# Moving the conversion of a weight chunk behind the next step's row turn after a small slot

## The chip, the core and the metric

The kernel runs on one core of a Trainium2 chip. The metric is the device time of one execution in microseconds (us). The engines work side by side, each through its own queue in order: TensorE (PE in the rows; PEld is its weight loading), VectorE (DVE), ScalarE (ACT), GpSimd (POOL) and SyncE (SP, which only issues DMA transfers here). "DVEq" and the like name an engine's sequencer: branches and semaphore events, not work.

## The reference, cut to what matters

Three stages follow each other: windowed attention, a top-1 mixture of experts (MoE) whose expert is sometimes held from one token to the next, and a gated feed-forward layer with a convolution. The change lies in the MoE stage and touches the weights of the third.

```python
# MoE: d_model 512, 8 experts, d_ff 1024, 4 x 544 tokens
e = fresh_e if s == 0 or local_gate[b, s] < 0.5 else prev_e
h = np.maximum(x[b, s] @ w1[e], 0.0)
out[b, s] = p[e] * (h @ w2[e])
# third stage
h = np.maximum(x @ w_in, 0.0)
gate = 1.0 / (1.0 + np.exp(-conv(h, conv_w)))
return h * gate @ w_out
```

The weights w_in and w_out (and conv_w) arrive with 8 bytes per number; the kernel brings them to 4-byte floats itself, with integer operations.

## The kernel before, in words

The MoE stage sorts the tokens by expert into **slots** of 128 rows; a slot holds one expert only. `Moe.run` (L1186) runs slots 2 to 20 by `step(s)` (L1406), one step per slot, and slot 21 by `last`. Every matmul is done in three products of high and low parts: a float tile is split into a high part (by ScalarE, a cast) and a low part (by VectorE, a subtraction). So a step on TensorE is: layer 1 of slot s, the row turn of slot s+1 (`turn_x`: four transposes; ScalarE writes xh, VectorE xl), layer 2 of slot s-1, the turn of the hidden rows of slot s (`turn_h`; ScalarE writes gh, VectorE gl).

Where the expert changes from slot s to s+1, its weights, loaded by SyncE into ws (`fetch`, L1280), are split: W1 by `resplit(s + 1, 1)` in step s (four pieces), W2 by `resplit(s + 1, 2)` at the end of step s+1 (eight pieces, W2 of slot s by `resplit(s, 2)` in step s). Both lie in a conditional block on `chg` of the slot (L1295), which every engine passes, taken or not; the registers come from the routing table `esi`, row 1. A slot with at most 32 rows is **small** (row 5 of `esi`): its two layers are computed straight from the unsplit weights and take TensorE about 2 us each in place of 5.6.

Beside this, sixteen **chunks** of the third stage's weights are converted, one a step. `raw_load` (L1442) brings chunk s-2 into one of two buffers in step s. Chunk c = s-3 is converted in step s by `conv64` (L1007): six operations on VectorE (L1011 to L1016), one addition on GpSimd (L1017), and a last operation on VectorE, here called the **tail** (L1018), which is returned as a function and run a step later, in the `while self.conv` loop right behind the row turn. Where the expert stays from s to s+1, the six operations stand early in the step (block of L1424, ahead of layer 2, the hidden turn and the W2 split); where it changes, at the step's end (block of L1436). The engines' queues follow the order in which the code is written; nothing reorders them.

In this data the slots with a changed expert are 4, 7, 9, 13, 16, 18 and 21; small slots that `step` runs are 2, 9, 13 and 16. After 9, 13 and 16 the next slot keeps the expert.

Of the kernel before, what the change touches and what calls it, by code (L numbers as in the profile page):

```python
# [13 lines left out]
ALU = mybir.AluOpType  # L14
# [545 lines left out]
NA = 2  # L560
NB = NSLOT - NA
# [94 lines left out]
class Routing:  # L656
# [15 lines left out]
    def tl(self, shape, name, dt=F32, tag=None):  # L672
        return self.rp.tile(shape, dt, name=name, tag=tag or name)
# [170 lines left out]
    def phase_b(self, rp, pst):  # L844
        nc, c, tl = self.nc, self.c, self.tl
        v = nc.vector
        self.rp = rp
        yield from self.front(1, pst)
        n = NT
# [40 lines left out]
        sc = tl([1, NB], "r_sc")  # L890
# [24 lines left out]
        esi = self.esi  # L915
        ch = tl([1, NB], "r_ch")
# [8 lines left out]
        va = tl([1, NB], "r_va")  # L925
# [4 lines left out]
        v.tensor_tensor(esi[:, 3, NA + 1:], va[:, 1:], ch[:, 1:], ALU.mult)  # L930
        v.tensor_scalar(esi[:, 2, NA:], ni, 7, None, ALU.bitwise_and)
        v.tensor_copy(esi[:, 4, 0:1], inc[0:1, 7:8])
        yield

    def few(self, b0, first):
# [71 lines left out]
def conv64(nc, raw, out):  # L1007
    hi, lo = raw[:, :, 1], raw[:, :, 0]
    v = nc.vector
    a = out.bitcast(I32)  # L1010
    v.tensor_scalar(a, hi, 3, 0x7FFFFFFF, ALU.logical_shift_left, ALU.bitwise_and)  # L1011
    v.scalar_tensor_tensor(a, hi, -2 ** 31, a, ALU.bitwise_and, ALU.bitwise_or)
    v.tensor_scalar(hi, hi, 1, 21, ALU.logical_shift_left, ALU.logical_shift_right)
    v.tensor_scalar(hi, hi, 897.0, -1.0, ALU.is_ge, ALU.mult)
    v.scalar_tensor_tensor(a, lo, 29, a, ALU.logical_shift_right, ALU.bitwise_or)
    v.tensor_scalar(lo, lo, 28, 1, ALU.logical_shift_right, ALU.bitwise_and)  # L1016
    nc.gpsimd.tensor_tensor(a, a, lo, ALU.add)  # L1017
    return lambda: v.scalar_tensor_tensor(a, a, 0x40000000, hi, ALU.bitwise_xor, ALU.bitwise_and)  # L1018
# [33 lines left out]
class Moe:  # L1052
    def __init__(self, sig, tc, W, ident, x_dram, y_dram, rt, w1, w2, wi, wo):
        self.nc, self.tc = tc.nc, tc
        self.W, self.ident, self.x_dram, self.y_dram = W, ident, x_dram, y_dram
        self.rt, self.w1, self.w2, self.wi, self.wo = rt, w1, w2, wi, wo
        self.sig = sig
        self.xs, self.xt, self.ht, self.hs, self.next, self.chg, self.sm = {}, {}, {}, {}, {}, {}, {}
        self.conv, self.raw = [], {}

    def open(self, ctx):
        self.ctx = ctx
# [146 lines left out]
    def last(self, s, cwr, cw):  # L1209
        nc, W, f2 = self.nc, self.W, self.f2  # L1210
        hp, hs = self.h_tile(), self.tp.tile([P, FF], F32, tag="hs", name="hs")
        xt, ht = self.xt.pop(s), {}
        w, y = W.t[1], {}
        ht = tuple(self.tp.tile([P, NFC, P], F32R, tag="g" + x, name="g" + x) for x in "hl")

        def split(a, b):
            for k in range(a, b):
                W.split_k(1, W.f, k, nc.gpsimd if k in POOL_K[1] else nc.vector)

        def resplit(a, b):  # L1220
            with self.tc.If(self.chg[s] != 0):
                for k in range(a, b):
                    W.split_k(2, W.s, k, nc.gpsimd if k in POOL_L else nc.vector)

        for k in range(K_LAST):
            self.l1_mm(xt, w, hp, k, range(2))
        split(0, K_LAST)
        nc.scalar.activation(self.sig, self.sig, AF.Sigmoid)
        self.layer2(s - 1)
        self.fetch(s - 1, 2)  # L1230
        f2.load0()
        resplit(0, 4)
        for k in range(K_LAST, NKC - 1):
            self.l1_mm(xt, w, hp, k, range(2))
        self.conv_w(cwr, cw)
        self.rt.late_flag(s + 1, self.ps.tile([P, 4, P], F32, tag="tr", name="lf")[0:1, 0, 0:1])
        t = []
        for c in range(2):
            self.l1_mm(xt, w, hp, NKC - 1, (c,))
            self.relu_c(hp, hs, c)  # L1240
        for a in (0, 4):
            t.append(self.hi_t(hs, ht, a, self.ps))
        for a in (0, 4):
            self.lo_t(ht, a, t[a // 4])
        resplit(4, NFC)
        yp = self.y_tile()
        for k in range(NFC):
            self.l2_mm(ht, W.t[2], yp, k)
            for f in PREP0.get(k, ()):
                if f < 10:  # L1250
                    (f2.scale0 if f < 5 else f2.xt0)(f % 5, self.ps)
                else:
                    split(f - 10, f - 9)
        self.out(s, yp)
# [30 lines left out]
        self.W.load(n, (self.w1, self.w2)[n - 1][bass.ds(e, 1)], **({"cond": c} if (s, n) != (0, 1) else {}))  # L1285

    def changed(self, s, pool=False):
        return self.nc.values_load(self.rt.esi[0:1, 1, s:s + 1], min_val=0, max_val=1,
                                   engines=[mybir.EngineType.Activation, mybir.EngineType.Pool]
                                   + ([] if pool else [mybir.EngineType.DVE]))  # L1290

    def resplit(self, s, n, eng=None):
        if n == 1 or s < NA:
            self.chg[s] = self.changed(s, eng is not None)
        with self.tc.If(self.chg[s] != 0):  # L1295
            self.W.split(n, self.W.s, eng)

    def small(self, s):
# [107 lines left out]
    def step(self, s):  # L1406
        W, hi = self.W, NSLOT - 3
        if s + 1 < hi - 1:
            self.small(s + 1)
        self.layer1(s)  # L1410
        self.fetch(s, 1)
        if s + 3 < hi:
            self.xs[s + 3] = self.gather(s + 3)
        if s + 1 < hi - 1:
            self.turn_x(s + 1)
        else:
            self.xt[s + 1] = self.hi_lo_t(self.xs.pop(s + 1), NKC, "x")
        while self.conv:
            self.conv.pop()()
        if s < NA + 16:  # L1420
            self.raw_load(s - NA)
        self.resplit(s + 1, 1)
        if NA < s <= NA + 16:
            with self.tc.If(self.chg[s + 1] == 0):  # L1424
                self.convert(s - NA - 1)
        if s == NA:
            for _ in self.rest:
                pass
        else:
            self.layer2(s - 1)  # L1430
            self.fetch(s - 1, 2)
        self.turn_h(s)
        self.resplit(s, 2)
        if NA < s <= NA + 16:
            self.conv.pop()
            with self.tc.If(self.chg[s + 1] != 0):  # L1436
                self.convert(s - NA - 1)

    def chunk(self, s):
        return (1, s // 2, 512 * (s % 2)) if s < 8 else (2, s - 8, 0)  # L1440
# [6 lines left out]

    def convert(self, s):
        n, k, o = self.chunk(s)
        self.conv.append(conv64(self.nc, self.raw[s], self.W.f[n][:, k, o:o + 512]))  # L1450


class Ffn2:
# [411 lines left out]
```

## Time and profile before

| | us |
|---|---|
| time, median of three runs | 630.27 (627.69 to 630.58) |
| profiled execution | 626.94 |
| its span | 624.9 |
| TensorE busy in the span | 579.3 (93%) |
| VectorE busy | 416.5 (67%) |
| ScalarE busy | 318.2 (51%) |
| GpSimd busy | 176.5 (28%) |

The steps of the MoE stage run from about 180 to 394 us of the span, `last` to about 416, and the third stage from about 421 on. Busy shares are means over stages with different limits: within a step it counts which engine another one waits for. A timeline row gives start, duration, engine, line, operation, output and inputs, and in brackets the idle time ahead of it and what ended it.

### The profile page before, as it was taken

To read this page: it belongs to the slowest core of one execution; us is meant where nothing else is said; L and a number is where in the kernel's file an instruction comes from. 1 tells how busy PE (TensorE), PEld (TensorE's weight loads), DVE (VectorE), ACT (ScalarE), POOL (GpSimd) and SP (SyncE) were. 2 spreads that over 40 slices of the span, in tenths; PEclk is the share of its full clock that TensorE was granted. 3 is DMA by queue.
4 is the path that set the end of the run, shared out by engine and by line. 5 is a ranking of instruction groups with operands and counts; after the bars stand their busy time and mean duration, and the time that the engine had idled before them with its cause. 6 is when DMAs were issued, how large, how long until landed. Compare 5 with 4: busy or idle time off the path is not lost. (4 is left out here: it accounts for less than half of the span.)

```text
span 624.9 us, 16315 instructions
## 1 busy us (share of the span) xinstructions
PE 579.3 (93%) x6066; PEld 484.7 (78%) x6066; DVE 416.5 (67%) x868; ACT 318.2 (51%) x634; POOL 176.5 (28%) x226
## 2 busy tenths in 40 slices
PE   8779898889989999989989899969999999999997
PEld 7567676666758888768767688749998998998986
DVE  7868577866965878784878884578984384383330
ACT  5755545574225455443545654656864463463341
POOL 7665820042031423333243330100132243300100
PEclk9999989999899999989999899998999999999999
DMA  9989968558049575774558474123101201000001
GB/s 232 208 172 263 258 127 196 201 178 287 20 128 335 206 242 205 250 255 162 216 172 289 158 254 153 38 75 85 50 15 37 85 2 50 35 2 35 34 35 51
DMA packets 60643, 90.56 MB, mean 145 GB/s; under 512 B 25726, under 2 KB 34198, under 8 KB 60504
## 3 DMA queue, kind: packets, MB, share of 16 engines
q1 hardware_dynamic: 57016, 78.93, 41.7%
q0 software_dynamic: 3520, 10.23, 4.8%
q8 instruction: 64, 1.05, 0.7%
q14 instruction: 43, 0.35, 0.2%
HBM read 125.87 MB, written 15.79 MB: 227 GB/s over the span
## 5 line engine op out<-in xcount | busy, mean ns | idle before, releaser
L1569 DVE SCALAR_TENSOR_TENSOR fc<-f_hp,cw,fc 128x544 f32<-128x544 f32 (+2 forms) x66 | 51.1, 775 | 70.7 <-ACT fc L1567 69.3
L1045 DVE TENSOR_TENSOR wl<-ws,wh 128x512 fp32r<-128x512 f32 (+1 forms) x92 | 74.3, 868 | 12.5 <-ACT wh L1044 11.8
L1044 ACT CAST wh<-ws 128x512 fp32r<-128x512 f32 (+1 forms) x96 | 66.3, 772 | 2.0 <-DMA ws<-in_moe_w_dram 0.9
L1125 PE MATMUL yp<-wh,gh 128*128 128x512 f32 x144 | 58.9, 409 | 1.1 <-ACTq L1295 0.9
L1125 PE MATMUL yp<-wl,gh 128*128 128x512 f32 x144 | 57.0, 396 | 0.7 <-DVEq L1295 0.7
L1125 PE MATMUL yp<-wh,gl 128*128 128x512 f32 x144 | 57.0, 396 | 0.0
L1109 PE MATMUL hp<-wl,xh 128*128 128x512 f32 x144 | 47.5, 402 | 8.6 <-DVEq L1295 5.4
L1627 PE MATMUL f<-wh,fh 128*128 128x512 f32 (+1 forms) x144 | 54.8, 380 | 0.0
L1627 PE MATMUL f<-wh,fl 128*128 128x512 f32 (+1 forms) x144 | 54.4, 378 | 0.0
L1627 PE MATMUL f<-wl,fh 128*128 128x512 f32 (+1 forms) x144 | 54.4, 378 | 0.0
L1082 POOL DMA_INDIRECT y_dram<-ys,sidx x22 | 25.4, 1156 | 95.8 <-ACT ys L1401 46.7
L1273 ACT ACTIVATE hs<-hp 128x512 f32<-128x512 f32 x36 | 19.9, 595 | 61.1 <-PE hp L1109 61.1
L278 ACT ACTIVATE pr<-sp,nm 128x128 f32<-128x128 f32 x128 | 36.6, 375 | 26.4 <-DVE nm L275 26.4
L1109 PE MATMUL hp<-wh,xh 128*128 128x512 f32 x144 | 49.2, 413 | 0.1
L1109 PE MATMUL hp<-wh,xl 128*128 128x512 f32 x144 | 47.8, 404 | 0.0
L1070 POOL DMA_INDIRECT xs<-x_dram,gidx x22 | 26.9, 1225 | 64.6 <-ACT pr L278 34.1
L1017 POOL TENSOR_TENSOR wf<-wf,fx 128x512 int32<-128x512 int32 x16 | 20.9, 1304 | 74.4 <-DVE fx L1016 66.0
L1109 PEld LDWEIGHTS hp<-wl,xh 128*128 128x128 f32 x144 | 27.2, 192 | 16.3 <-DVEq L1295 6.7
L1574 ACT ACTIVATE f_hp<-f 128x544 f32<-128x544 f32 x31 | 19.4, 626 | 36.8 <-PE f L1550 36.7
L1636 ACT COPY fy<-f 128x512 f32<-128x512 f32 (+1 forms) x18 | 10.1, 564 | 47.1 <-PE f L1627 47.1
L1401 ACT COPY ys<-yp 128x512 f32<-128x512 f32 x15 | 8.9, 592 | 48.7 <-PE yp L1125 42.4
L1109 PEld LDWEIGHTS hp<-wh,xl 128*128 128x128 f32 x144 | 27.7, 193 | 6.4 <-DVE xl L1102 0.3
(380 smaller groups left out, 1525.6 us busy)
## 6 DMA issues: line engine op xcount, KB each, us to landing
ws<-in_moe_w_dram SPq DMA_DIRECT2D x42, 2048.0 KB
fx<-y_dram SPq DMA_DIRECT2D x17, 256.0 KB
raw<-in_k_l_dram SPq DMA_DIRECT2D x16, 256.0 KB
x_dram<-x SPq DMA_DIRECT2D x16, 256.0 KB
fx<-in_moe_w_in_dram SPq DMA_DIRECT2D x8, 512.0 KB
fx<-in_moe_w_out_dram SPq DMA_DIRECT2D x8, 512.0 KB
out_dram<-fy SPq DMA_DIRECT2D x16, 256.0 KB
VA<-in_v_l_dram SPq DMA_DIRECT2D x20, 192.0 KB
```

The source lines that it names most:

```text
L278: nc.scalar.activation(pr[:, hp, :], sp[:, hp, :], AF.Exp, bias=nm[:, hp:hp + 1], scale=-1.0)
L1017: nc.gpsimd.tensor_tensor(a, a, lo, ALU.add)
L1044: (cp.tensor_copy if cp else self.nc.scalar.copy)(h, src[n][:, k, :])
L1045: eng.tensor_tensor(l, src[n][:, k, :], h.bitcast(F32), ALU.subtract)
L1070: self.nc.gpsimd.indirect_dma_start(out=xs, out_offset=None, in_=self.x_dram[0:n, :], in_offset=bass.IndirectOffsetOnAxis(ap=self.rt.gidx[ ...
L1082: self.nc.gpsimd.indirect_dma_start(out=self.y_dram[:, :], out_offset=bass.IndirectOffsetOnAxis(ap=self.rt.sidx[:, s:s + 1], axis=0), in_= ...
L1109: self.nc.tensor.matmul(hp[c], a[:, k, :], b[:, 512 * c:512 * c + 512], start=k == 0 and m == 0, stop=k == NKC - 1 and m == 2)
L1125: self.nc.tensor.matmul(yp, a[:, k, :], b, start=k == 0 and m == 0, stop=k == NFC - 1 and m == 2)
L1273: self.nc.scalar.activation(hs[:, 512 * c:512 * c + 512], hp[c], AF.Relu)
L1569: nc.vector.scalar_tensor_tensor(c[:, a:b], hp[:, a + t:b + t], self.cw[:, t, f:f + 1], c[:, a:b], ALU.mult, ALU.add)
L1574: self.nc.scalar.activation(hp[:, 1:S + 1].rearrange("p (a c) -> p a c", a=2), p[:, :, 0:272], AF.Relu)
L1627: self.nc.tensor.matmul(yp[:, cs], x[:, c], w[:, cs], start=f == 0 and n == 0, stop=f == NFC - 1 and n == 2)
```

## The change

The routing table's row 1 gets a third value: a slot that keeps its expert after a small slot that changed it has 2 (four operations on one partition at the end of `phase_b`). The blocks that split weights now ask for `== 1` in place of `!= 0`, so 2 counts as unchanged there.

The tail of a chunk moves from the loop behind the row turn into a new `convert_early`, behind `resplit(s + 1, 1)`. There, a step whose own value is 2 runs the whole conversion of the chunk before (six operations, addition, tail); any other runs the tail of the chunk before and then, as before, the six operations of its own chunk if `chg` of the next slot is 0. `convert_end` at the step's end runs the own chunk if `chg` of the next slot is 1 or the own value is 2. A small slot's step whose next slot has value 2 thus converts nothing. `raw_load` moves behind `convert_early`.

```diff
@@ phase_b
+        sc = tl([1, NB], "r_sc")
+        v.tensor_tensor(sc, ch, esi[:, 5, NA:], ALU.mult)
+        v.tensor_scalar(va, ch, -2.0, 2.0, ALU.mult, ALU.add)
+        v.tensor_tensor(sc[:, 0:NB - 1], sc[:, 0:NB - 1], va[:, 1:], ALU.mult)
+        v.tensor_tensor(esi[:, 1, NA + 1:], sc[:, 0:NB - 1], ch[:, 1:], ALU.add)
@@ resplit (and the same in last)
-        with self.tc.If(self.chg[s] != 0):
+        with self.tc.If(self.chg[s] == 1):
             self.W.split(n, self.W.s, eng)
@@ step
-        while self.conv:
+        while s > NA + 17 and self.conv:
             self.conv.pop()()
+        self.resplit(s + 1, 1)
+        self.convert_early(s)
         if s < NA + 16:
             self.raw_load(s - NA)
-        self.resplit(s + 1, 1)
-        if NA < s <= NA + 16:
-            with self.tc.If(self.chg[s + 1] == 0):
-                self.convert(s - NA - 1)
...
         self.turn_h(s)
         self.resplit(s, 2)
-        if NA < s <= NA + 16:
-            self.conv.pop()
-            with self.tc.If(self.chg[s + 1] != 0):
-                self.convert(s - NA - 1)
+        self.convert_end(s)
+
+    def convert_early(self, s):
+        c = s - NA - 1
+
+        def own():
+            if 0 <= c < 16:
+                with self.tc.If(self.chg[s + 1] == 0):
+                    self.convert(c)
+
+        if 0 < c <= 16:
+            with self.tc.If(self.chg[s] == 2) as i:
+                self.convert(c - 1)
+                self.tails[c - 1]()
+            with i.Else():
+                self.tails[c - 1]()
+                own()
+        else:
+            own()
+
+    def convert_end(self, s):
+        c = s - NA - 1
+
+        def own():
+            with self.tc.If(self.chg[s + 1] == 1):
+                self.convert(c)
+
+        if 0 < c < 16:
+            with self.tc.If(self.chg[s] == 2) as i:
+                self.convert(c)
+            with i.Else():
+                own()
+        elif c == 0:
+            own()
@@ convert
-        self.conv.append(conv64(self.nc, self.raw[s], self.W.f[n][:, k, o:o + 512]))
+        self.tails[s] = conv64(self.nc, self.raw[s], self.W.f[n][:, k, o:o + 512])
```

VectorE in a step before, behind the row turn (xl): wf is the converted chunk, fx its raw buffer, wl and ws the low part and the unsplit W1.

```order
L1102 TENSOR_TENSOR xl<-xlp,xh 128x512
L1304 UNCONDITIONAL_BRANCH
L1018 SCALAR_TENSOR_TENSOR wf_3965<-wf_3965,fx 128x512
L1288 TENSOR_LOAD esi
L1295 COMPARE_AND_BRANCH
L1045 TENSOR_TENSOR wl_0_2726<-ws_3447,wh_0_2725 128x1024
...
L1295 UNCONDITIONAL_BRANCH x2
L1424 COMPARE_AND_BRANCH
L1011 TENSOR_SCALAR wf_3965<-fx 128x512
```

The same place of the changed kernel, where lines stand five lower in the file:

```order
L1107 TENSOR_TENSOR xl<-xlp,xh 128x512
L1309 UNCONDITIONAL_BRANCH
L1293 TENSOR_LOAD esi
L1300 COMPARE_AND_BRANCH
L1050 TENSOR_TENSOR wl_0_2726<-ws_3447,wh_0_2725 128x1024
...
L1300 UNCONDITIONAL_BRANCH x2
L1448 COMPARE_AND_BRANCH
L1016 TENSOR_SCALAR wf_3970<-fx 128x512
...
L1021 TENSOR_SCALAR fx<-fx 128x512
L1023 SCALAR_TENSOR_TENSOR wf_3970<-wf_3970,fx 128x512
L1448 UNCONDITIONAL_BRANCH
L1023 SCALAR_TENSOR_TENSOR wf_3970<-wf_3970,fx 128x512
L1444 COMPARE_AND_BRANCH
```

The tail (L1018, now L1023) stands behind the block of the W1 split and twice: at the end of the put-off conversion (the block of L1448) and, in the other branch, alone ahead of the own conversion (L1444).

SyncE in a step before: the raw load (fx) ahead of the blocks, the W2 load (ws) behind them.

```order
L1446 DMA fx<-in_moe_w_in_dram 128x1024 [waits DMAHW7_49,DVE_49]
L1295 UNCONDITIONAL_BRANCH
L1424 UNCONDITIONAL_BRANCH
L1304 UNCONDITIONAL_BRANCH x2
L1037 ISA
L1037 DMA ws_2724<-in_moe_w_dram 128x8x512 [waits DMAHW3_49,PE_49,Activation_49]
```

And changed:

```order
L1300 UNCONDITIONAL_BRANCH
L1448 UNCONDITIONAL_BRANCH
L1309 UNCONDITIONAL_BRANCH x2
L1479 DMA fx<-in_moe_w_in_dram 128x1024 [waits DMAHW7_49,DVE_49,Pool_49]
L1042 ISA
L1042 DMA ws_2724<-in_moe_w_dram 128x8x512 [waits DMAHW3_49,PE_49,Activation_49]
```

The raw load now comes behind the conversion's block and waits for GpSimd too; the W2 load still follows it in the queue.

## Rows read from the trace of the kernel before

**Rows 1.** Timeline of TensorE: second matmul of layer 1, slots 11, 15, 18.

```profile
275.94 0.72 PE L1109 MATMUL hp<-wl,xh 128*128 128x512 f32 x2 [2.21 <-DVEq L1295]
...
321.69 0.73 PE L1109 MATMUL hp<-wl,xh 128*128 128x512 f32 x2 [2.09 <-DVEq L1295]
...
354.60 0.79 PE L1109 MATMUL hp<-wl,xh 128*128 128x512 f32 x2 [3.11 <-DVE wl L1045]
```

**Rows 2.** Table by stage: us, busy of each engine, then PEclk, DMA share, GB/s.

```profile
243.34:248.92 5.58, 5.58 (x27) 4.54 (x26) 5.01 (x9) 5.18 (x11) 1.98 (x2) 1.00 0.59 227
273.03:282.67 9.64, 7.43 (x25) 5.58 (x26) 6.14 (x11) 1.13 (x3) 2.32 (x2) 0.82 0.67 211
318.89:326.81 7.92, 5.83 (x25) 4.46 (x25) 6.03 (x11) 1.23 (x3) 1.61 (x2) 1.00 0.54 170
350.78:361.31 10.53, 7.42 (x25) 5.59 (x26) 8.60 (x11) 3.97 (x8) 1.41 (x1) 0.84 0.69 221
420.00:427.00 7.00, 6.13 (x28) 6.16 (x28) 5.50 (x10) 2.50 (x5) 0.28 (x6) 0.51 0.56 133
```

**Rows 3.** Timeline of VectorE, from step 9 into step 10.

```profile
264.28 0.43 DVE L1011 TENSOR_SCALAR wf<-fx 128x512 int32<-128x512 int32 x1 [0.41 <-DVEq L1295]
...
267.00 0.43 DVE L1016 TENSOR_SCALAR fx<-fx 128x512 int32<-128x512 int32 x1
267.99 5.59 DVE L1045 TENSOR_TENSOR wl<-ws,wh 128x512 fp32r<-128x512 f32 x8 [0.57 <-PE hp L1109]
274.54 0.69 DVE L1102 TENSOR_TENSOR xl<-xlp,xh 128x512 fp32r<-128x512 f32 x1 [0.95 <-ACTq L1295]
275.14 0.68 DVE L1018 SCALAR_TENSOR_TENSOR wf<-wf,fx 128x512 int32<-128x512 int32 x1
```

**Rows 4.** Timeline of GpSimd: the addition of the conversion in step 9.

```profile
267.51 1.30 POOL L1017 TENSOR_TENSOR wf<-wf,fx 128x512 int32<-128x512 int32 x1 [2.68 <-DVEq L1304]
```

**Rows 5.** Who waited for whom, TensorE, 165 to 425 us: total, times, longest.

```profile
PE yp L1125 <- DVEq L1295: 0.7, 1, 0.7
```

**Rows 6.** Timeline of TensorE: second matmul of layer 2, slots 10, 12, 15, 17.

```profile
283.34 0.40 PE L1125 MATMUL yp<-wl,gh 128*128 128x512 f32 x1
...
304.44 0.39 PE L1125 MATMUL yp<-wl,gh 128*128 128x512 f32 x1
...
336.30 0.39 PE L1125 MATMUL yp<-wl,gh 128*128 128x512 f32 x1
...
361.98 0.40 PE L1125 MATMUL yp<-wl,gh 128*128 128x512 f32 x1
```

**Rows 7.** Timeline of ScalarE: casts of W2 in step 9, of W1 in step 17.

```profile
265.57 4.27 ACT L1044 CAST wh<-ws 128x512 fp32r<-128x512 f32 x8 [0.73 <-DMA ws<-in_moe_w_dram]
...
348.74 3.90 ACT L1044 CAST wh<-ws 128x1024 fp32r<-128x1024 f32 x4
```

**Rows 8.** Timeline of SyncE: raw load and W2 load of step 8.

```profile
251.95 0.34 SPq L1446 DMA_DIRECT2D fx<-in_moe_w_in_dram  x1
255.14 3.21 SPq L1037 DMA_DIRECT2D ws<-in_moe_w_dram  x2
```

**Rows 9.** Timeline of VectorE: tail in step 8, gl in 12, W1 split in 17.

```profile
251.23 0.69 DVE L1018 SCALAR_TENSOR_TENSOR wf<-wf,fx 128x512 int32<-128x512 int32 x1 [1.22 <-DVEq L1304]
...
302.78 1.29 DVE L1102 TENSOR_TENSOR gl<-hlp,gh 128x512 fp32r<-128x512 f32 x2 [0.53 <-ACTq L1295]
...
353.32 4.62 DVE L1045 TENSOR_TENSOR wl<-ws,wh 128x1024 fp32r<-128x1024 f32 x4
```

**Rows 10.** Timeline of VectorE, steps 14 and 15: xl, tail, gl of slot 15.

```profile
320.29 0.69 DVE L1102 TENSOR_TENSOR xl<-xlp,xh 128x512 fp32r<-128x512 f32 x1 [0.95 <-ACTq L1295]
...
328.40 0.69 DVE L1018 SCALAR_TENSOR_TENSOR wf<-wf,fx 128x512 int32<-128x512 int32 x1 [1.91 <-POOLq L1424]
...
334.77 1.29 DVE L1102 TENSOR_TENSOR gl<-hlp,gh 128x512 fp32r<-128x512 f32 x2 [0.53 <-ACTq L1295]
```

**Rows 11.** Timeline of VectorE: xl of slot 2, behind the routing.

```profile
179.88 0.69 DVE L1102 TENSOR_TENSOR xl<-xlp,xh 128x512 fp32r<-128x512 f32 x1 [1.58 <-ACT xh L1327]
```

More of the change, by code (lines that the diff above doesn't have):

```diff
@@ L1058, in __init__ @@
         self.xs, self.xt, self.ht, self.hs, self.next, self.chg, self.sm = {}, {}, {}, {}, {}, {}, {}
-        self.conv, self.raw = [], {}
+        self.conv, self.raw, self.tails = [], {}, {}
     def open(self, ctx):
@@ L1287, in changed @@
     def changed(self, s, pool=False):
-        return self.nc.values_load(self.rt.esi[0:1, 1, s:s + 1], min_val=0, max_val=1,
+        return self.nc.values_load(self.rt.esi[0:1, 1, s:s + 1], min_val=0, max_val=2,
                                    engines=[mybir.EngineType.Activation, mybir.EngineType.Pool]
@@ L1294, in resplit @@
             self.chg[s] = self.changed(s, eng is not None)
-        with self.tc.If(self.chg[s] != 0):
+        with self.tc.If(self.chg[s] == 1):
             self.W.split(n, self.W.s, eng)
```

## Prediction

> **What bounds the kernel now.** The waits of TensorE in the expert stretch (165 to 425 us) were read first. The long ones all stand in front of the second matmul of a layer 1, the one that reads the low part of W1: 2.21 us at 275.94, 2.09 at 321.69 and 3.11 at 354.60 [rows 1]. These are layer 1 of slots 11, 15 and 18. Slots 9, 13 and 16 ran small: each of the three comes two steps after a small slot. That matmul may go only when VectorE has passed the row turn of its slot (xl) and the W1 split's block, taken or not.
>
> A table by stage then gives the price [rows 2]. An undisturbed layer 1 with its first turn takes 5.58 us; the three take 9.64, 7.92 and 10.53. The excess is 4.06 + 2.34 + 4.95 = 11.35 us, of which 7.41 is waiting. Most of the rest is clock: the first and third stretch were granted 0.82 and 0.84, so (1 - 0.82) x 9.64 = 1.74 and (1 - 0.84) x 10.53 = 1.68 us went to the lower level; the second ran at 1.00.
>
> What ends last is on VectorE. In step 9 [rows 3] it converts chunk 6 (six operations from 264.28 to 267.43, 3.15 us), then splits W2 (267.99 to 273.58), then turns xl of slot 11 (274.54 to 275.23), then runs the tail of chunk 6 (to 275.82); TensorE goes at 275.94. So VectorE is late by the conversion, and the change aims at the right thing. After 362 us TensorE works without such waits, so what it loses or wins up to there passes to the end.
>
> **The change, part by part.** *Taken away.* In steps 9, 13 and 16 the early conversion leaves the place ahead of the W2 split. In every step the tail leaves the place between xl and TensorE's release. If nothing else were late, all 11.35 us would come back.
>
> *Put in instead.* In steps 10, 14 and 17 the whole conversion now runs behind the row turn and the W1 block, in one piece: six operations 3.15, then VectorE stands until GpSimd's addition is done (it starts 0.08 after the sixth and takes 1.30 [rows 4]; 0.1 for the signal), then the tail 0.68. That is 5.3 us; before, the 1.4 us of GpSimd lay under other work. Behind this piece on VectorE stands gl, the low part of the hidden rows of the same step, and TensorE needs that for the second matmul of the next layer 2: its only wait there put down to VectorE in before is 0.7 us [rows 5]. The old places of this second matmul are 283.34, 304.44, 336.30 and 361.98 [rows 6]. So the question is when gl comes, not when xl comes.
>
> *Step 10.* Without the conversion the W2 split of step 9 hangs on ScalarE's casts, which start at 265.57 after a wait of 0.73 for the W2 load [rows 7]. That load moves. On SyncE the raw load goes at 251.95 and the W2 load behind it at 255.14 [rows 8]; the raw load goes as the tail of chunk 4 ends (251.23 + 0.69 [rows 9]). Now the tail stands behind the W1 split of step 8 (four pieces, 4.62 [rows 9]): about 251.9 + 4.6 + 0.2 + 0.5 = 257.2, and W2 can go only about 257.9, 2.8 us later. How much later it lands no row shows: nothing at best, 2.8 at worst; I take 1.8, nearer the worst, since the rows show the split's casts waiting for this very load. xl of slot 11 then ends at 272.6 (best), 275.3 (worst), 274.1 (taken), against 275.23. Conversion and gl follow: 0.3 + 5.3 + 0.3 + 1.3 + 0.2 = 7.4, so gl is passed at 281.5. TensorE, relieved of 4.06, would ask at 283.34 - 4.06 = 279.3 and waits 2.2. Gain here: 283.34 - 281.5 = **1.85** (3.3 to 0.6).
>
> *Step 12, and 8 and 15 alike.* In a step whose next slot changes expert, the tail now runs between the W1 split and gl instead of ahead of the split, where VectorE had idled. gl of slot 12 starts 302.78 and lasts 1.29 [rows 9], done 304.07; with 0.68 and about 0.2 more it is done 304.95, against 304.44. Loss **0.5**, 0.3 to 0.9. (In step 8 the same lies inside the bounds above, in step 15 inside the next sum.)
>
> *Steps 13 to 15.* Here VectorE is the bound. Before, from the end of xl of slot 15 (320.98) to the end of gl of slot 15 (336.06) lie 15.1 us [rows 10] with almost no idle time, and TensorE's second matmul follows at 336.30. After, xl comes 3.15 + 1.3 (won so far: 1.85 - 0.5) earlier, at 316.5. But the stretch now holds one conversion more (3.15) and the exposed GpSimd wait (1.5): 19.7 us. gl ends at 336.2. TensorE would come at 336.3 - 1.3 - 2.3 = 332.7 and waits 3.6. **Net against before, at this point: 0.0.** The work was moved, not removed, and what it was moved in front of is just as awaited.
>
> *Steps 16 and 17.* The W1 split of slot 18 started at 353.32 [rows 9]; freed of the conversion it hangs on ScalarE's casts (from 348.74, four in 3.90 [rows 7]) and runs 349.9 to 354.5. TensorE's wait of 3.11 is gone. Then 0.3 + 5.3 + 0.4 + 1.3 + 0.1: gl of slot 17 at 361.9, against 361.98. TensorE would come at 361.98 - 4.95 = 357.0 and waits 4.8. **Net at this point: -0.1**, with +-1.5 for the gaps at branches, of which the rows show 0.53, 1.22 and 1.91 [rows 9, 10].
>
> *The clock.* Before, the waits of 2.21 and 3.11 were followed by the lower level (1.2 GHz), the one of 2.09 was not [rows 1, 2]. The new waits are longer, 3.6 and 4.8. I charge 1.7 for the longer and half of it for the other: **+2.6** (0 to 5).
>
> *At no cost.* The four routing operations on one partition come ahead of an idle time of 1.58 us, in which VectorE waits for ScalarE's xh [rows 11]; without it they would cost some 0.7. Raw loads wait in every step for VectorE's and GpSimd's part of the block, up to 4 us longer, but their chunk is read a step (12 us) later. The W2 load for slot 18 goes some 7 us later, behind the raw load of step 17; the casts that read it come some 8 us after that. Bound: nothing to 1.
>
> Sum: -1.85 + 0.5 back to 0.0, then -0.1, then +2.6 = **+2.5 us**. On the profiled execution's 626.94 us that is 629.4; the median of the runs shown, 630.27, lies 3.3 above that execution, so the forecast is 632.8.
>
> The gaps on VectorE where a small slot's turn is jumped over are 1.22 and 1.91 us [rows 9, 10]. The Trainium skill (Runtime: NRT & Kernel Launch, Instruction fetch mechanics) says that a taken branch out of the prefetched pages waits for a fetch; the change makes the jumped-over blocks longer. The Trainium skill (Advanced Engine Details and Errata, Control Flow Timing) gives about 0.11 us for a compare-and-branch and 0.05 for a plain one: two nested levels more on each of the four spots above would be an estimated 0.6 us, and the sum +3.1 rather than +2.5 if none of it were in the gaps taken. The rows' gaps are longer than such prices add up to, and by the first rule each could grow; no row here shows by how much.
>
> **The rivals.** *A, faster:* the put-off conversion stays hidden. That needs gl of slot 17 before 357.0 and gl of slot 15 before 332.7, which means that VectorE would have to save 3 to 5 us at the branches or that layer 2 did not wait for gl. Against it: VectorE has no idle time to give. For it: layer 2 shows just one such wait. With some 1 us lost in steps 8 and 12, the gain would be half to nearly all of the 11.35: -5 to -9, 621 to 625. Chance 0.12.
>
> *B, slower:* the clock decides. If both new waits are followed by the lower level, the second for as long as between 420 and 427 us, where TensorE ran 7 us at 0.51 [rows 2] and lost (1 - 0.51) x 7 = 3.4, the charge is 1.7 + 3.4 = 5.1 and the time 635.3; with one stretch each, 3.4, and W2 landing at its worst, 634.5. It decides from where the charge exceeds 3.2 us. Chance 0.36.
>
> *C, nothing happens:* the flag 2 is never set, because no small slot that changes expert is followed by a slot of the same one. Against it: the early conversion at 264.28, ahead of a W2 split, shows just that case. Only the reordering would be left, +1, 631.3. Chance 0.04.
>
> **How the numbers follow.** The forecast (give-back on gl plus one to two low-clock stretches, 0 to +3.1) has 0.48. Within 0.5% (3.2 us, about what a measurement of this kernel can tell from no change) are the forecast and C: 0.52. Slower is B: 0.36; faster is A: 0.12. The forecast's own range is 630 to 633.4. The range for 8 in 10 reaches into B, 628.0 to 636.5, and leaves out A and the far end of B; runs of before alone span 2.9 us.
>
> **What the profile would show.** Right: no wait at the second matmul of layer 1 of slots 11, 15 and 18; new waits of some 2, 3.5 and 5 us at the second matmul of layer 2 of slots 10, 15 and 17, put down to VectorE; low clock right behind at least one of them; the six operations, GpSimd's addition and the tail in one row behind xl in steps 10, 14 and 17; the W2 load of step 8 about 3 us later. Wrong: layer 2 starting without a wait there, or full clock throughout.

## The result, and the profile after

The changed kernel takes 635.0 us (median of six runs, 632.3 to 640.5) against 629.4 for the kernel before in the same comparison; ratio 1.0103, 95% interval 1.0056 to 1.0151. It is slower by 1%. Forecast was 632.8, within 0.5% of before, with 635.3 and "slower" as rival B. The time lies inside the range for 8 in 10 (628.0 to 636.5) and outside the forecast's own (630 to 633.4).

| profiled execution | before | after |
|---|---|---|
| time, span (us) | 626.94, 624.9 | 632.31, 630.3 |
| layer 1 of slot 2 begins | 179.49 | 178.13 |
| third stage, first matmul with weights | 420.87 | 426.51 |
| between the two: "expert stretch" | 241.38 | 248.38 |

The stretch is the better measure in single profiles: its start moves by some us from run to run, with nothing in the code ahead of it changed but the four routing operations. By it the change costs 7.0 us.

Who waited for whom on TensorE in this stretch (total, times, longest):

```profile
PE yp L1130 <- DVEq L1300: 12.0, 7, 3.9
PE hp L1114 <- DVEq L1300: 1.1, 1, 1.1
PE hp L1114 <- DVE wl L1050: 0.3, 1, 0.3
```

Lines stand five lower than in before. The waits of layer 1 [rows 1] are gone, and the 0.7 us of layer 2 [rows 5] have become 12.0. The second matmuls of layer 2 that answer to [rows 6], TensorE's timeline (start, length, idle time ahead and what ended it); they are slots 8, 10, 12, 14, 15 and 17:

```profile
260.10 0.50 PE L1130 MATMUL yp<-wl,gh 128*128 128x512 f32 x1 [2.61 <-DVEq L1300]
...
283.06 0.50 PE L1130 MATMUL yp<-wl,gh 128*128 128x512 f32 x1 [0.28 <-DVEq L1300]
...
305.47 0.50 PE L1130 MATMUL yp<-wl,gh 128*128 128x512 f32 x1 [1.02 <-DVEq L1300]
...
326.96 0.50 PE L1130 MATMUL yp<-wl,gh 128*128 128x512 f32 x1 [0.48 <-DVEq L1300]
...
339.09 0.50 PE L1130 MATMUL yp<-wl,gh 128*128 128x512 f32 x1 [3.06 <-DVEq L1300]
...
365.68 0.79 PE L1130 MATMUL yp<-wl,gh 128*128 128x512 f32 x1 [3.89 <-DVEq L1300]
```

And the clock there (us, busy time of PE, PEld, DVE, ACT, POOL, then PEclk, DMA share, GB/s), behind the waits of slots 8, 15 and 17:

```profile
256.60:267.32 10.72, 8.11 (x35) 6.34 (x32) 7.24 (x12) 0.97 (x3) 3.04 (x3) 0.84 0.79 255
333.28:343.28 10.00, 6.94 (x50) 4.79 (x50) 7.90 (x13) 1.83 (x4) 2.99 (x3) 0.84 0.80 273
360.96:372.00 11.04, 7.15 (x23) 5.54 (x22) 8.12 (x16) 1.56 (x3) 5.05 (x4) 0.69 0.59 196
```

Reckoned as in the prediction, the time lost to the lower level is (1 - 0.84) x 10.72 = 1.72, then 1.60, then (1 - 0.69) x 11.04 = 3.42 us, where before lost 1.74 + 1.68 = 3.4 [rows 2]. For slot 17 this is too much, since the level fell while TensorE still waited and had nothing to lose:

```profile
364.00:365.68 1.68, 0.00 (x1) 0.00 (x1) 1.57 (x3) 0.00 (x0) 1.19 (x1) 0.50 0.22 29
```

What the level cost is read from the time between the second matmul of layer 2 and the hidden turn behind it. At slot 17 that turn starts (TensorE, after, then before)

```profile
373.37 1.03 PE L1382 MATMUL hlp<-ident,hs 128*128 128x128 f32 x8
```

```profile
367.23 1.04 PE L1377 MATMUL hlp<-ident,hs 128*128 128x128 f32 x8
```

so 7.69 us behind 365.68, and in before 5.25 behind 361.98: 2.4 us. Slots 8 and 15 give 1.6 and 1.7 in the same way, 5.8 in all.

Laid side by side, the lead or lag of after against before (start of the row of after less that of before) is -1.4 at the start of the stretch, **+1.7 at layer 2 of slot 8** (258.40 to 260.10), +3.3 at the turn of slot 11 (269.45 to 272.79), -0.3 at layer 2 of slot 10, +1.0 at slot 12, +2.8 at slot 15, +3.7 at slot 17, and +5.6 at the third stage. Two pieces were foreseen in kind (the gain of 3.6 up to slot 10, and its loss up to slot 17). The 3.1 us lost ahead of layer 2 of slot 8, with 1.6 more just behind it, were not: no conversion is put off there.

**Step 7, where it begins.** GpSimd, SyncE, ScalarE and VectorE of after, in time order from 243 to 259 us:

```profile
243.52 1.31 POOL L1022 TENSOR_TENSOR wf<-wf,fx 128x512 int32<-128x512 int32 x1 [3.03 <-DVE fx L1021]
244.86 0.34 SPq L1479 DMA_DIRECT2D fx<-in_moe_w_in_dram  x1
245.54 0.08 SPq L1042 DMA_DIRECT2D ws<-in_moe_w_dram  x1
245.70 4.27 ACT L1049 CAST wh<-ws 128x512 fp32r<-128x512 f32 x8 [2.41 <-DMA ws<-in_moe_w_dram]
...
252.94 4.63 DVE L1050 TENSOR_TENSOR wl<-ws,wh 128x1024 fp32r<-128x1024 f32 x4 [1.67 <-PE yp L1130]
257.48 0.69 DVE L1023 SCALAR_TENSOR_TENSOR wf<-wf,fx 128x512 int32<-128x512 int32 x1
258.70 1.29 DVE L1107 TENSOR_TENSOR gl<-hlp,gh 128x512 fp32r<-128x512 f32 x2 [0.53 <-ACT xh L1332]
```

The same of before (SyncE, then ScalarE, then VectorE):

```profile
239.57 0.34 SPq L1446 DMA_DIRECT2D fx<-in_moe_w_in_dram  x1
242.85 0.08 SPq L1037 DMA_DIRECT2D ws<-in_moe_w_dram  x1
...
244.24 4.28 ACT L1044 CAST wh<-ws 128x512 fp32r<-128x512 f32 x8
...
256.99 1.29 DVE L1102 TENSOR_TENSOR gl<-hlp,gh 128x512 fp32r<-128x512 f32 x2 [0.53 <-ACTq L1295]
```

The raw load stands behind the conversion's block, one arm of which reads the buffer that it refills. It therefore waits for whatever arm ran, here the step's *own* conversion with GpSimd's addition: 243.52 + 1.31 = 244.83, raw load at 244.86. The W2 fetch of the step follows on SyncE at 245.54, and ScalarE's casts of W2 start 0.16 us behind that. This fetch brings nothing: it carries a condition, which holds only where the slot before it changed expert; it takes 0.08 us of issue, where the one at 258.98 that loads takes 0.39; and from 244.80 to 249.00 us 185 GB/s moved, 0.8 MB, about the raw chunk (0.5) and the rows that GpSimd scatters (0.26), where W2 has 2.1. But it is the last in code order on that buffer, and the casts start right behind it all the same. Casts 2.4 us late make the W2 split, the W1 split of slot 9 and the tail late, then gl, and TensorE stands 2.61 us and runs at the lower level behind it.

### The profile page after: what moved, and what is told of

It is laid out like the page before. It is cut to its first block, busy times and chain, and to the rows that moved or that the text cites. A ratio compares the mean times of both kernels' runs of the same rounds, so it can differ in the third digit from the quotient of the medians.

```text
span 630.3 us, 16384 instructions
## 1 busy us (share of the span) xinstructions
PE 579.8 (92%) x6066; PEld 483.7 (77%) x6066; DVE 417.2 (66%) x872; ACT 317.2 (50%) x634; POOL 174.8 (28%) x226
## 3 DMA queue, kind: packets, MB, share of 16 engines
q8 instruction: 64, 1.05, 0.7%
## 5 line engine op out<-in xcount | busy, mean ns | idle before, releaser
L1050 DVE TENSOR_TENSOR wl<-ws,wh 128x512 fp32r<-128x512 f32 (+1 forms) x92 | 72.2, 848 | 25.5 <-ACT wh L1049 21.7
L1130 PE MATMUL yp<-wl,gh 128*128 128x512 f32 x144 | 59.7, 414 | 12.4 <-DVEq L1300 12.0
L1130 PE MATMUL yp<-wh,gh 128*128 128x512 f32 x144 | 60.3, 419 | 1.1 <-ACTq L1300 0.9
L1130 PE MATMUL yp<-wh,gl 128*128 128x512 f32 x144 | 58.9, 409 | 0.0
L1114 PE MATMUL hp<-wh,xl 128*128 128x512 f32 x144 | 46.2, 392 | 0.0
L1130 PEld LDWEIGHTS yp<-wl,gh 128*128 128x128 f32 x144 | 28.4, 197 | 20.6 <-DVEq L1300 14.2
L1130 PEld LDWEIGHTS yp<-wh,gh 128*128 128x128 f32 x144 | 28.5, 198 | 7.1 <-ACTq L1300 1.1
```

The lines of the kernel that those rows point to most:

```text
L1050: eng.tensor_tensor(l, src[n][:, k, :], h.bitcast(F32), ALU.subtract)
L1114: self.nc.tensor.matmul(hp[c], a[:, k, :], b[:, 512 * c:512 * c + 512], start=k == 0 and m == 0, stop=k == NKC - 1 and m == 2)
L1130: self.nc.tensor.matmul(yp, a[:, k, :], b, start=k == 0 and m == 0, stop=k == NFC - 1 and m == 2)
```

## Experiments

Each kernel was compared with before on the same chip. "Stretch" is the expert stretch of its one profile (before 241.38, after 248.38).

| kernel | us, median | ratio to before [95%] | stretch |
|---|---|---|---|
| after | 635.0 | 1.0103 [1.0056, 1.0151] | 248.4 |
| reorder_only | 636.4 | 1.0117 [1.0092, 1.0142] | 251.5 |
| third_raw | 628.4 | 1.0002 [0.9972, 1.0032] | 242.2 |
| w2_first | 628.9 | 1.0021 [0.9991, 1.0051] | 241.9 |
| third_noflag | 629.6 | 1.0038 [1.0001, 1.0075] | 243.2 |
| no_putoff | 618.7 | 0.9818 [0.9785, 0.9850] | 232.9 |
| putoff_end | 628.6 | 0.9986 [0.9959, 1.0013] | 245.3 |
| tail_late | 625.3 | 0.9960 [0.9933, 0.9987] | 238.8 |
| wh_first | 627.0 | 0.9967 [0.9938, 0.9995] | 238.7 |
| late_wh | 621.0 | 0.9880 [0.9847, 0.9913] | 233.8 |
| before_wh | 622.8 | 0.9948 [0.9917, 0.9979] | 235.7 |
| late_wh12 | 620.4 | 0.9873 [0.9813, 0.9932] | 235.3 |

Two theories stood against each other. **P**: the put-off piece in front of gl costs what it gains, and the clock on top (the forecast and rival B). **L**: the moved raw load holds up SyncE.

### The reordering alone

```diff
-        sc = tl([1, NB], "r_sc")
-        v.tensor_tensor(sc, ch, esi[:, 5, NA:], ALU.mult)
...
-        v.tensor_tensor(esi[:, 1, NA + 1:], sc[:, 0:NB - 1], ch[:, 1:], ALU.add)
```

> The changed kernel with the four routing operations left out: no slot ever has the value 2, so nothing is put off and only the moved tail, the moved raw load and the two branch levels are left. Theory P (the put-off piece in front of gl costs): 630 to 631, no wait over 1 us at the second matmul of layer 2, the three old waits of layer 1 (2.2, 2.1, 3.1) back. Theory L (the raw load now waits until VectorE is past the W1 split and the tail, and holds up the W2 load behind it on SyncE, whose casts come late): the wait of 2.6 at layer 2 of slot 8 and the low clock behind it stay, about 4.3 us, so 633.5 to 635; ScalarE's casts still wait over 2 us for the W2 load in step 7.

As L has it, and 1.4 us worse: 636.4, no less than the changed kernel, with nothing put off. TensorE's wait at layer 2 of slot 8, and what ScalarE waited for the fetches in the expert stretch:

```profile
260.09 0.50 PE L1125 MATMUL yp<-wl,gh 128*128 128x512 f32 x1 [2.97 <-DVEq L1295]
```

```profile
ACT wh L1044 <- DMA ws<-in_moe_w_dram: 22.8, 9, 4.9
```

In the changed kernel ScalarE's row is 8.8 us. So the reordering by itself costs as much as the whole change; the put-off gives at most a little of it back. ScalarE waits longer here because steps 9, 13 and 16 convert early, as in before, and then the raw load holds up the fetch there too; in the changed kernel these steps convert nothing.

### SyncE freed, in two ways

third_raw gives the raw chunks 0 to 13 a third buffer and puts the load back:

```diff
+        if s < NA + 14:
+            self.raw_load(s - NA)
         self.resplit(s + 1, 1)
         self.convert_early(s)
-        if s < NA + 16:
+        if NA + 14 <= s < NA + 16:
             self.raw_load(s - NA)
@@ raw_load
-        raw = self.raw[s] = self.f2.fx[s % 2].bitcast(I32).rearrange("p (n t) -> p n t", t=2)
+        b = 2 if s % 3 == 2 and s < 14 else s % 3 if s < 14 else s % 2
+        raw = self.raw[s] = (self.f2.fx[b] if b < 2 else self.W.f[2][:, 6:8, :].rearrange("p k f -> p (k f)")).bitcast(I32).rearrange("p (n t) -> p n t", t=2)
```

> The changed kernel with a third raw buffer for chunks 0 to 13 (in a part of the target of chunks 14 and 15 that is not yet written), so that the raw load goes back ahead of the W1 split and waits for nothing; the put-off conversion and the tail stay where the change put them. Theory P: 634 to 635, since gl still stands behind the put-off piece; waits of some 3 and 4 us at layer 2 of slots 15 and 17 stay. Theory L: W2 of slots 7, 9, 13 and 16 is issued 3 to 8 us earlier, ScalarE's 8.8 us of waiting for ws fall below 2, the wait at layer 2 of slot 8 and its low clock go (4.3 us), the one at slot 17 falls from 3.9 to about 2: 627 to 629.

w2_first keeps two buffers and moves the raw load once more:

```diff
         else:
             self.layer2(s - 1)
             self.fetch(s - 1, 2)
+        if s < NA + 16:
+            self.raw_load(s - NA)
```

> The changed kernel, two raw buffers, with the raw load moved once more: behind the W2 load on SyncE. Theory L (the W2 loads held up behind the raw load cost the 6 us between the changed kernel and the one with a third buffer): the W2 load of step 6 goes at about 230, not 235, the wait at layer 2 of slot 8 falls from 2.6 to under 1 and its low clock goes; raw chunks land later, behind 2 MB, which may hold VectorE up in steps 7 and 18 by 0 to 3 us: 628 to 632. Against it (the third buffer helped by something else, say by freeing VectorE of waits for GpSimd): 634 to 636.

Both land at 628.4 to 628.9, the time of before: by the ratios, 5 to 6 us come back. The fetch of step 7 in third_raw, its cast, and in the same kernel the waits at slots 15 and 17 (SyncE, ScalarE, TensorE), then ScalarE's waiting in all:

```profile
241.89 0.08 SPq L1042 DMA_DIRECT2D ws<-in_moe_w_dram  x1
243.28 4.28 ACT L1049 CAST wh<-ws 128x512 fp32r<-128x512 f32 x8
...
333.86 0.79 PE L1130 MATMUL yp<-wl,gh 128*128 128x512 f32 x1 [3.05 <-DVEq L1300]
...
360.33 0.50 PE L1130 MATMUL yp<-wl,gh 128*128 128x512 f32 x1 [3.90 <-DVEq L1300]
```

```profile
ACT wh L1049 <- DMA ws<-in_moe_w_dram: 0.3, 1, 0.3
```

The cast no longer waits, and of slot 8's wait 0.29 is left. Of the 6.2 us between the two stretches (248.38 less 242.21), 3.9 lie at slot 8 (2.3 of waiting, 1.6 of clock), 0.7 is a shorter low stretch behind slot 17 (second matmul to hidden turn in 6.96 us, not 7.69), and the rest is in small waits at slots 10 to 15. Where L was wrong: slot 17's wait stayed at 3.90 and did not fall to 2. ScalarE's W2 casts of step 16 stand in its queue behind its copy of layer 2 of slot 15, and that comes late because of the wait at slot 15:

```profile
340.98 0.59 ACT L1406 COPY ys<-yp 128x512 f32<-128x512 f32 x1 [9.78 <-PE yp L1130]
...
341.73 4.27 ACT L1049 CAST wh<-ws 128x512 fp32r<-128x512 f32 x8
```

So behind slot 15 ScalarE's own queue, and not SyncE, sets when these casts begin. That a shorter wait at slot 15 would by itself shorten slot 17's is not shown: in putoff_end below the two are 3.47 and 3.75.

### The put-off without the loads

third_noflag is third_raw with the four routing operations left out (the diff of reorder_only).

> As third_raw, but with the four routing operations left out, so that nothing is put off: the raw load is free of all waits, and only the tail and the branches are moved. Against third_raw it shows the put-off alone. If the give-back on gl is complete, as the prediction's sum had it (0.0 at layer 2 of slot 15, -0.1 at slot 17, clock +2.6): 626 to 629, equal to third_raw or up to 2.6 under it. If the put-off wins and the load alone had hidden it: 632 to 634.

Measured 629.6 against third_raw's 628.4 (ratios 1.0038 and 1.0002, whose intervals overlap; stretches 243.2 and 242.2). The waits of layer 1 are back at slots 11, 15 and 18 (TensorE):

```profile
278.58 0.73 PE L1109 MATMUL hp<-wl,xh 128*128 128x512 f32 x2 [1.65 <-DVEq L1295]
...
323.12 0.73 PE L1109 MATMUL hp<-wl,xh 128*128 128x512 f32 x2 [1.94 <-DVEq L1295]
...
358.12 1.22 PE L1109 MATMUL hp<-wl,xh 128*128 128x512 f32 x2 [0.78 <-DVE wl L1045]
```

But the pair does not show the put-off alone, as had been expected. In both kernels only the raw loads up to step 15 go early. third_noflag converts early in step 16, so there the raw load waits for GpSimd's addition (348.62), the fetch goes behind it at 349.31, and ScalarE, then TensorE, wait:

```profile
349.46 4.26 ACT L1044 CAST wh<-ws 128x512 fp32r<-128x512 f32 x8 [4.90 <-DMA ws<-in_moe_w_dram]
```

```profile
354.75 1.09 PE L1377 MATMUL hlp<-ident,hs 128*128 128x128 f32 x8 [3.10 <-ACT hs L1273]
```

third_raw converts nothing in that step and has no such wait. These 3.1 us belong to L. What the put-off gains or costs by itself is therefore not shown, only that no large gain of it was hidden.

### The put-off conversions left out

```diff
             with self.tc.If(self.chg[s] == 2) as i:
-                self.convert(c - 1)
-                self.tails[c - 1]()
+                n, k, o = self.chunk(c - 1)
+                self.nc.gpsimd.memset(self.W.f[n][:, k, o:o + 512], 0.0)
```

> The changed kernel with the put-off conversions of chunks 6, 10 and 13 left out (their targets are set to zero by GpSimd), so that part of the third stage's weights is missing: an upper bound of what the put-off piece costs. Theory P: all new waits at layer 2 of slots 10, 14, 15 and 17 go, 9 to 12 us under the changed kernel, 623 to 626, and layer 2 of slot 8 waits no more than 1 us. Theory L: the same at slots 15 and 17, but the 2.6 us at slot 8 with the low clock behind it stay and ScalarE still waits some 5 to 9 us for ws: 626 to 628.

At 618.7 it lies below what either theory gave. It was no clean bound: without the put-off arm nothing behind the W1 split reads the raw buffer, so the raw load waits for the tail only (step 7: raw load at 245.53, GpSimd's addition at 248.61), SyncE runs ahead and slot 8 waits 0.30 us. It bounds P and L together, at 16 us under the changed kernel.

### Put off still further

putoff_end is third_raw with, up to step 15, the put-off conversion at its step's end, behind gl.

```diff
+            if s < NA + 14:
+                with self.tc.If(self.chg[s] != 2):
+                    self.tails[c - 1]()
+                    own()
+                return
@@ convert_end, arm of the value 2
+                if s < NA + 14:
+                    self.convert(c - 1)
                 self.convert(c)
+                if s < NA + 14:
+                    self.tails[c - 1]()
```

> As third_raw, but in steps up to 15 the put-off conversion stands at the end of its step, behind gl and together with the step's own one (tail behind both, so that GpSimd's addition is hidden); step 17 stays as in the changed kernel. Theory P: gl of slots 10 and 14 comes 5 us earlier, their waits go, the one of slot 15 falls from 3.1 to about 1.5: 632 to 633. Theory L: below third_raw by 1 to 2 us, 626 to 627.

628.6, the same as third_raw: below P's 632 to 633 and above L's 626 to 627. Slot 15 waits 3.47 us, not P's 1.5 (in a profiled execution of 630.76, 2 us above the median). Between xl and gl of slot 15 the same conversions lie on VectorE wherever they stand; what is left to try is taking work out of that stretch, or asking for gl later.

### Tail behind gl; TensorE asks later

tail_late is third_raw with every tail behind the hidden turn, once for both arms; the raw loads of steps 16 and 17 move there with it, behind the W2 fetch:

```diff
             with self.tc.If(self.chg[s] == 2) as i:
                 self.convert(c - 1)
-                self.tails[c - 1]()
             with i.Else():
-                self.tails[c - 1]()
                 own()
@@ step
         self.turn_h(s)
+        if 0 < s - NA - 1 <= 16:
+            self.tails[s - NA - 2]()
+        if NA + 14 <= s < NA + 16:
+            self.raw_load(s - NA)
```

> As third_raw, but the tail of every step stands behind the hidden turn (gl), once for both branches; so gl no longer waits for GpSimd's addition in steps 10, 14 and 17 (2.1 us) nor for the tail in steps 8, 12 and 15 (0.7 to 1.1). Theory P (gl behind the put-off piece is what is left of the cost): the wait at slot 15 falls from 3.05 to about 2, the one at slot 17 from 3.9 to about 1.5, perhaps with one stretch of low clock less: 3 to 5 us under third_raw, 623 to 626. If instead VectorE's sum of work alone sets the end: the same as third_raw, 628 to 629.

625.3, as P has it, though its interval and third_raw's just overlap; slot 17 waits longer than the 1.5 expected. Slots 15 and 17 (TensorE):

```profile
334.70 0.50 PE L1130 MATMUL yp<-wl,gh 128*128 128x512 f32 x1 [1.21 <-DVEq L1300]
...
358.61 0.50 PE L1130 MATMUL yp<-wl,gh 128*128 128x512 f32 x1 [2.57 <-DVEq L1300]
```

wh_first leaves VectorE as in third_raw and changes the order of layer 2's matmuls:

```diff
             for k in range(NFC):
-                self.l2_mm(h, W.t[2], yp, k)
+                self.l2_mm(h, W.t[2], yp, k, (0,))
+            for k in range(NFC):
+                self.l2_mm(h, W.t[2], yp, k, (1, 2))
```

> As third_raw, but the full layer 2 runs its eight matmuls with the high part of W2 and gh first, then the sixteen others; nothing on VectorE changes. Only the point at which TensorE must wait moves, 1.6 us later. Theory P: the waits at slots 15 and 17 fall to about 1.4 and 2.3 and what follows them is 1.6 to 3.5 us earlier each, more where the low clock goes too: 623 to 626. If the low clock comes from the wait being there, whatever its length, both stretches stay: 625 to 626.

627.0, a gain of 1.4 us over third_raw where 2.4 to 5.4 were expected, and not clear of noise: the two waits are 2.26 and 2.33, and low clock follows the first only. The order has a price of its own at slot 18, whose W2 is still being cast: the eight matmuls go no faster than ScalarE's casts and take 3.31 us, and layer 2 takes 6.8 up to the hidden turn, where third_raw's takes 5.6 (TensorE):

```profile
373.48 3.31 PE L1132 MATMUL yp<-wh,gh 128*128 128x512 f32 x8
```

late_wh is third_raw with both of these diffs.

> Both together: third buffer, tail behind gl, high products of layer 2 first. Theory P: no wait over 1 us at layer 2 of slots 10 to 17 and no low clock between 330 and 370 us; the whole of the two waits (3.05 + 3.9) and of the low clock behind them (about 3.7) comes back, less what turns up next: 618 to 622, clearly under both kernels. If VectorE's sum sets the end: 626 to 628.

Both together take 621.0, 1.2% under before and 14 us under the changed kernel, and in the profiled execution, the fastest of the six, the high level holds from 200 us to the end of the stretch but for the last pause ahead of the third stage. The one wait over 1 us left at layer 2 of slots 8 to 17 (TensorE, slot 17) and the stretch behind it:

```profile
356.11 0.50 PE L1132 MATMUL yp<-wl,gh 128*128 128x512 f32 x1 [1.42 <-DVEq L1302]
```

```profile
356.00:366.00 10.00, 9.89 (x47) 8.26 (x48) 8.31 (x16) 5.73 (x11) 3.94 (x5) 1.00 0.81 296
```

### The same order of matmuls in the kernel before

```diff
@@ layer1, full
             for k in range(NKC):
-                self.l1_mm(x, W.t[1], hp, k, range(2))
+                self.l1_mm(x, W.t[1], hp, k, range(2), (0,))
+            for k in range(NKC):
+                self.l1_mm(x, W.t[1], hp, k, range(2), (1, 2))
```

and layer 2 as in wh_first.

> The kernel before, nothing put off or moved, but the full layers 1 and 2 run all their matmuls of the high parts first (8 each) and the others behind them. The three waits at layer 1 of slots 11, 15 and 18 (2.21, 2.09, 3.11) should fall by about 1.4 each, the low clock behind the first and perhaps the third with them: 4.2 to 7.6 us, 621 to 625. If the order of the matmuls only helps together with the put-off: 627 to 629.

```profile
276.44 0.73 PE L1109 MATMUL hp<-wl,xh 128*128 128x512 f32 x2 [1.10 <-DVEq L1297]
...
319.25 0.72 PE L1109 MATMUL hp<-wl,xh 128*128 128x512 f32 x2 [0.50 <-DVEq L1297]
...
351.56 0.73 PE L1109 MATMUL hp<-wl,xh 128*128 128x512 f32 x2 [1.78 <-DVE wl L1045]
```

622.8, without any work moved: the waits of [rows 1] shrink from 2.21, 2.09 and 3.11 to these, and no low clock follows them. So the order alone, here in both layers, gives 0.5% of late_wh's 1.2%. The put-off, the third buffer and the moved tail together give the rest, 0.7% (0.9880 against 0.9948). late_wh12 adds the order in layer 1 to late_wh:

> late_wh with the high products first in layer 1 too. There layer 1 of slot 16 and 17 waits 0.6 at most: 0 to 1 us under late_wh, 620 to 621. More than that only if the order itself costs or saves something on TensorE.

620.4, no different from late_wh by its interval.

## Why the prediction was right or wrong, point by point

**What bounds: right.** The waits of layer 1 came from the conversion and are gone.

**Step 10: right in kind, the size off.** Up to layer 2 of slot 10 the changed kernel gained 3.6 us from the turn of slot 11 on (+3.3 to -0.3), foreseen 1.85; gl was asked for 0.28 us early, not 2.2. Counted from the start of the stretch (-1.4 to -0.3) it had lost 1.1 by there, because of slot 8. The piece itself ran as costed (VectorE, and GpSimd's addition in it):

```profile
275.40 0.69 DVE L1107 TENSOR_TENSOR xl<-xlp,xh 128x512 fp32r<-128x512 f32 x1 [0.94 <-ACTq L1300]
276.42 0.43 DVE L1016 TENSOR_SCALAR wf<-fx 128x512 int32<-128x512 int32 x1 [0.33 <-DVEq L1300]
...
279.65 1.30 POOL L1022 TENSOR_TENSOR wf<-wf,fx 128x512 int32<-128x512 int32 x1 [4.30 <-DVE fx L1021]
280.99 0.69 DVE L1023 SCALAR_TENSOR_TENSOR wf<-wf,fx 128x512 int32<-128x512 int32 x1 [1.42 <-POOL wf L1022]
281.67 1.29 DVE L1107 TENSOR_TENSOR gl<-hlp,gh 128x512 fp32r<-128x512 f32 x2
```

From 276.42 to 281.67 are 5.25 us, 5.3 in the sum. TensorE was late itself, behind slot 8. (A slip in the sum: 1.8 us on the best 272.6 is 274.4, not 274.1.)

**The raw load and the W2 fetch: the step that failed.** The prediction wrote that the wait of 0.73 for the W2 load [rows 7] was for the load issued in step 8 [rows 8]. It was for the fetch of step 9 itself; before's SyncE has it at

```profile
265.41 0.08 SPq L1037 DMA_DIRECT2D ws<-in_moe_w_dram  x1
```

and the cast began at 265.57, 0.16 later, the same 0.16 as in step 7 above. In the changed kernel the load of step 8 goes at 258.98, and the casts of step 9 again wait 0.72, up to 0.17 behind their own fetch at 268.73. So the late landing of the load of step 8 was no cost, while "Raw loads wait in every step ..., but their chunk is read a step (12 us) later" (under *At no cost*) was the real one: not the chunk is late but the fetch queued behind it. And "In step 8 the same lies inside the bounds above" was mis-sized: the wait there is 2.61, with 1.6 of clock, where 0.5 (0.3 to 0.9) was the size for such a step. The undoing of this alone returned 5 to 6 us, twice.

The Trainium skill (DMA: Bandwidth & Descriptors, Rules for kernel authors) advises to issue a DMA early and wait on its semaphore late. The runs agree, and sharpen it: in the changed kernel the issue itself is late (245.54 against 241.89 in third_raw), since SyncE first waits out another transfer's buffer.

**Steps 12 to 15: right at slot 15, too small at slot 12.** Slot 12: loss 1.3 (-0.3 to +1.0) for 0.5 foreseen, beyond its 0.9. Slot 15: the wait is 3.06, foreseen 3.6. With SyncE freed, third_raw stands 2.44 us ahead of before at layer 2 of slot 15 and started its stretch 1.05 ahead: a net gain of 1.4 where the sum had 0.0.

**Steps 16 and 17: right.** Wait 3.89, foreseen 4.8; in third_raw net gain 0.6 at this point (1.65 less 1.05), foreseen 0.1.

**The clock: the kind right, the size under.** Slots 15 and 17 cost 1.73 + 2.44 = 4.2, not 2.6 and not rival B's 5.1, though inside the 0 to 5 given. That B's 635.3 met the time is partly luck: its clock is real, but slot 8 had no place in it, and third_raw, which loses 1.6 and 1.7 behind the same two waits, is no slower than before. The forecast too was nearer in time than in change: 1% of 629.4 is 6.5 us, where it had +2.5.

**The branches: not settled.** gl of slot 15 stood 0.53 behind its forerunner before [rows 10] and stands 0.81 behind it after (VectorE):

```profile
337.69 1.29 DVE L1107 TENSOR_TENSOR gl<-hlp,gh 128x512 fp32r<-128x512 f32 x2 [0.81 <-DVEq L1444]
```

This is 0.28 us, and at slot 12 it is 0.29. The Trainium skill (Advanced Engine Details and Errata, Control Flow Timing) gives 0.11 and 0.05 us for the two kinds of branch, so 0.27 is an estimate for two compares and a plain branch. The traces bear this out only in part: gl of slot 8, on the same path, stands 0.53 behind its tail (row of 258.70 above), and reorder_only, which has the same blocks, shows 0.53, 0.52 and 0.52 at slots 8, 12 and 15. So the number of branches does not explain the 0.28, and its cause stays open. At the turns that are jumped over no gap of several us turned up: those of 1.22 and 1.91 [rows 9, 10] are 1.67 and 1.32 after, now ahead of the W1 splits at 252.94 and 331.64.

**Rivals.** A (hidden anyway) fails on the waits of 3.06 and 3.89. C (nothing happens) fails on the put-off row in step 10; its price for the reordering alone, +1, was wrong as well: reorder_only took 1.2% more than before, over 7 us. The forecast's sum for what the put-off does, 0.0 to +2.5, agrees with third_raw (ratio 1.0002), which has the put-off and, beside it, a third buffer; the change also carried a second effect of 5 to 6 us.

## What to carry to other kernels

When a DMA is moved behind a block, look for what follows it on the issuing engine's queue, and for who waits on those, even a conditional load that brings nothing; a third buffer, or letting the load that others wait for go first, removes the wait. A piece of work moved off one wait lands in front of the next one on the same engine, so look first whether the waiting engine can ask later: here eight matmuls that need only the early operand, put first, gave as much (0.9948) as moving the work with both repairs (tail_late, 0.9960).

## What the runs showed of the hardware that had not been expected

The length of a wait of TensorE did not by itself tell whether the lower level follows. After a wait of 3.08 us in reorder_only the clock stayed at 1.00, after one of 1.99 us in late_wh12 it fell (TensorE, then the stretch behind it, for the one kernel and for the other):

```profile
324.02 1.09 PE L1377 MATMUL hlp<-ident,hs 128*128 128x128 f32 x8 [3.08 <-ACT hs L1273]
```

```profile
324.00:334.00 10.00, 9.49 (x46) 7.53 (x47) 5.87 (x11) 3.78 (x10) 3.07 (x3) 1.00 0.12 38
```

```profile
358.96 0.50 PE L1132 MATMUL yp<-wl,gh 128*128 128x512 f32 x1 [1.99 <-DVEq L1302]
```

```profile
358.00:368.00 10.00, 9.04 (x37) 7.37 (x38) 8.34 (x17) 3.43 (x7) 4.06 (x4) 0.83 0.77 288
```

third_noflag's wait of 3.10 at 354.75, the same operation waiting for the same one as in the first row here, was followed by 0.50 from 358 to 362 us. In wh_first, of two waits of 2.26 and 2.33 us the first was followed by it and the second was not. What decides it in this range stays open, so a charge for the clock behind a wait of 2 to 3 us can only be a range.
